# First chunk's q computed token tile by token tile and transposed by DMA, with the opening loads regrouped and GpSimd's order fixed

## The chip, the core and the metric

The kernel runs on one core of one Trainium2 chip. The metric is the device time of one execution in microseconds (us). Three runs of the kernel before took 745.28, 745.38 and 747.18 us; the median is 745.38 us.

## The reference

The input is one sequence of 2048 tokens by 1024 features, in bf16. Two residual blocks follow each other.

```python
def _A_ref(x, wqkv, wo):            # 32 heads of 32, window 8, dilation 2
    qkv = (x @ wqkv).reshape(B, S, 3, H, Dh)  # -> q, k, v
    ...
    logits = einsum('bhsd,bhswd->bhsw', q, kg) * scale   # kg: k of the tokens s, s-2, .. s-14
    o = einsum('bhsw,bhswd->bhsd', softmax(masked logits), vg)
    return o.reshape(B, S, D) @ wo
def _B_ref(x, w_in, w_sp, b_sp, w_out):
    z = gelu(x @ w_in)                        # 3584 columns: z1 | z2
    g = w_sp @ layernorm(z2) + b_sp           # mixing over the 2048 tokens
    return (z1 * g) @ w_out
h  = x + _A_ref(layernorm(x), wqkv, wo)
h2 = h + _B_ref(layernorm(h), w_in, w_sp, b_sp, w_out)
```

The change lies in the very first step: layernorm(x) and the q part of `x @ wqkv` for the first 512 tokens.

## The kernel before, in words

**Tiling.** The 2048 tokens are four chunks of 512 (`NCH`, `CH`); a chunk is four token tiles of 128 (`TPC`). The 1024 features are eight slices of 128 (`KT`). A product with 512 moving columns is one matmul instruction; 64 of them make q, k or v of one chunk.

**Opening (L202 to L267).** TensorE first runs 14 matmuls on a zero tile (`warm`, L206). SP's queue loads x tiles 0 and 1, ScalarE's queue loads tiles 3 and 2 (L210). Then SP loads wq in eight slices (L213), wk (L214), x tiles 4 to 7, wv (L217), and the other x tiles. An x buffer holds a pair of tiles, and there are four (`x4k`), so the tiles from 8 on wait until the `norm` of earlier tiles has read theirs. On GpSimd's queue the constants `csb` (among them the identity for transposes) are loaded first (L155). Each of the first four tiles goes through statistics (`stats` on VectorE; tile 3 in `stats_act` on ScalarE), a square root on ScalarE and a reciprocal (`rstd_of`), `norm`, eight transposes on TensorE and one copy out of PSUM (`xpose`). The result is `xnT[0]`, features on partitions and tokens along the free axis.

**q, k, v (`qkv`, L327).** For every chunk, weight slices are stationary and `xnT[c]` with its 512 tokens moves, so that the outcome has features on partitions. For q of chunk 0, four accumulators are filled together (L340), since a slice of wq is used as it arrives; all other groups run at L349. ScalarE copies chunk 0's q, k, v straight into `att_in[0]` (L356). For chunks 1 to 3 it copies to `stg` (L361), which SP stores to DRAM, and GpSimd's queue loads them again (L382) when the attention of the chunk before has let go of the buffers.

**Chunks 1 to 3 of x (`ln1`, L289).** VectorE takes statistics, GpSimd does one power (L298, 1/sqrt), VectorE does four `norm`s, GpSimd's queue writes them to DRAM (L304, `xn_d`), and SP brings them back transposed (`dma_start_transpose`, L309). The `xn` tiles and the `stg` tiles share four buffers.

**Attention (`attention`, L372).** VectorE multiplies q with shifted k (L405) and halves the sums (L409, L412); TensorE finishes the logits (L428); softmax runs on VectorE and ScalarE; two small matmuls spread the weights (L481); VectorE multiplies and adds over the window (L502, L508) into oT. `head` (L528) multiplies by wo (L550), adds x and normalizes. `b_z2` and `b_z1` (L623, L673) follow, and after L753 the token mixing (L771) and the output product (L788).

**What sets the order.** A planner written in the kernel (`Order`, L60) is given every operation with an engine, an assumed duration, dependences and a priority. It simulates the engines, from assumed starting clocks (L278: TensorE 12.9, ScalarE 12.0, VectorE 12.6) and assumed arrivals of x (`X_AT`, L286), and emits the operations by planned start. `manual_schedule` (L748) keeps that order on TensorE, ScalarE and VectorE. For the opening, and on SP's and GpSimd's queues throughout, a scheduler outside the kernel's text places the instructions. Every engine and every queue works strictly in its order: an instruction that waits holds up all behind it.

Of the kernel before, what the change touches and what calls it, by code (L numbers as in the profile page):

```python
# [20 lines left out]
P = 128  # L21
NT = S // P
CH = 512
# [9 lines left out]
NWARM = 14  # L33
# [7 lines left out]
def _consts():  # L41
    c = np.zeros((P, 128 + 32 + 128 + 128), np.float32)
    c[:, 0:128] = np.eye(P)
    for p in range(P):
        c[p, 128 + p // 4] = 1.0
    for k in range(P):
        h = k % 32
        c[k, 160 + 4 * h:160 + 4 * h + 4] = 1.0
    for w in range(W_WIN):
        for s in range(16):  # L50
            if s - DIL * w < 0:
                c[0:32, 288 + w * 16 + s] = NEG
    return c.astype(ml_dtypes.bfloat16)
# [70 lines left out]
def kernel(  # L124
# [18 lines left out]

    consts_d = nc.inline_tensor(_consts(), name="qt_consts")
# [16 lines left out]
    V.memset(eps_t[:], EPS)  # L161
    nhalf = cpool.tile([P, TPC], FP32, name="nhalf")
    V.memset(nhalf[:], -0.5)
# [29 lines left out]
    def x_slot(i):  # L193
        if i // 2 not in pairs:
            pairs[i // 2] = l1.tile([P, 2, D], BF16, name="xp", tag="x4k", bufs=4)
        xts[i] = pairs[i // 2][:, i % 2, :]

    def load_x(i):
        x_slot(i)
        dma(xts[i], x2d[i * P:(i + 1) * P, :])  # L200
# [4 lines left out]
    for _ in range(NWARM):  # L205
        T.matmul(wps[:], warm[:, 0:P], warm[:], start=True, stop=True)  # L206

    for i in (0, 3, 1, 2):
        x_slot(i)
        (dma if i < 2 else A.dma_start)(xts[i], x2d[i * P:(i + 1) * P, :])  # L210
    wsb = [wtile([P, KT, D], "wq", "wA"), wtile([P, KT, D], "wk", "wA"), wtile([P, KT, D], "wv", "wB")]
    for kt in range(KT):
        dma(wsb[0][:, kt, :], wq_view[:, kt, 0:D])  # L213
    dma(wsb[1][:], wq_view[:, :, D:2 * D])  # L214
    for i in range(TPC, 2 * TPC):
        load_x(i)
    dma(wsb[2][:], wq_view[:, :, 2 * D:3 * D])  # L217
    for i in range(2 * TPC, NT):
        load_x(i)
# [6 lines left out]

    def stats_act(i):
        sm = l1.tile([P, 4], FP32, name="sm", tag="sm")
        jk = l1.tile([P, D], BF16, name="jk", tag="xn", bufs=4)
        A.activation(jk[:], xts[i], ACTF.Identity, accum_out=sm[:, 0:1])  # L230
        A.activation(jk[:], xts[i], ACTF.Square, accum_out=sm[:, 1:2])
        V.tensor_scalar(mv1[:, i, 0:1], sm[:, 0:1], 1.0 / D, None, op0=ALU.mult)
        V.tensor_tensor(sm[:, 2:3], mv1[:, i, 0:1], mv1[:, i, 0:1], op=ALU.mult)
        V.scalar_tensor_tensor(mv1[:, i, 1:2], sm[:, 1:2], 1.0 / D, sm[:, 2:3], op0=ALU.mult, op1=ALU.subtract)
# [12 lines left out]

    def xpose(i, xn):
        tp = ps_acc.tile([P, KT, P], BF16, name="tpa", tag="acc")
        for a in range(KT):  # L250
            T.transpose(tp[:, a, :], xn[:, a * P:(a + 1) * P], ident)
        (V.tensor_copy if i == 2 else A.copy)(xnT[0][:, :, i * P:(i + 1) * P], tp[:])
# [3 lines left out]
    stats_act(3)  # L256
    stats(V, 0)
    rstd_of(0, 1)
    stats(V, 1)
    xpose(0, norm(0))  # L260
    rstd_of(1, 2)
    rstd_of(3, 4)
    xpose(1, norm(1))
    xpose(3, norm(3))
    stats(V, 2)
    rstd_of(2, 3)
    xpose(2, norm(2))  # L267
# [10 lines left out]
    o_ = Order({"PE": 12.9, "ACT": 12.0, "DVE": 12.6, "POOL": 12.0}, {"acc": 3, "L": 1, "prod": 2, "part": 2, "xn": 4})  # L278
# [7 lines left out]
    X_AT = {1: 18.5, 2: 27.5, 3: 30.5}  # L286
# [26 lines left out]
    att_in = {}  # L313

    def alloc_att_in(c):
        qT = att.tile([P, DLO, CH], BF16, name="qT", tag="qT")
        kT = att.tile([P, DLO, HALO + CH], BF16, name="kT", tag="kT")
        vT = att.tile([P, DLO, HALO + CH], BF16, name="vT", tag="vT")
        att_in[c] = (qT, kT, vT)

# [6 lines left out]
    def qkv(c):  # L327
        for xi in range(3):
            wv = wsb[xi][:].rearrange("p kt (m dl) -> p kt dl m", dl=DLO)
            for dp in range(DLO // 2):  # L330
                key = ("acc", "qkv", c, xi, dp)
                deps = [G.get(("xnT", c))]
                if c == 0 and xi == 0 and dp < 2:
                    def mm(wv=wv, dp=dp):
                        if dp == 0:
                            accs = [new_acc(), new_acc()]
                            G["acc", "qkv", 0, 0, 0], G["acc", "qkv", 0, 0, 1] = accs
                            for kt in range(KT):
                                for dl in range(4):
                                    T.matmul(accs[dl // 2][:, dl % 2, :], wv[:, kt, dl, :], xnT[0][:, kt, :],  # L340
                                             start=(kt == 0), stop=(kt == KT - 1))
                    last = add("PE", 6.91 if dp == 0 else 0.0, mm, deps, prio=order(), take="acc")
                else:
                    for j in range(2):
                        def mm(j=j, dl=2 * dp + j, wv=wv, key=key):
                            if j == 0:
                                G[key] = new_acc()
                            for kt in range(KT):
                                T.matmul(G[key][:, j, :], wv[:, kt, dl, :], xnT[c][:, kt, :],  # L349
                                         start=(kt == 0), stop=(kt == KT - 1))  # L350
                        last = add("PE", 1.727, mm, deps, prio=order(), take="acc" if j == 0 else None)
                        deps = [last]
                def ev(xi=xi, dp=dp, key=key):
                    if c == 0:
                        off = 0 if xi == 0 else HALO
                        A.copy(att_in[0][xi][:, 2 * dp:2 * dp + 2, off:off + CH], G[key][:])  # L356
                        if xi > 0 and dp == 3:
                            dma(qkv_d[xi][:, :, CH - HALO:CH], att_in[0][xi][:, :, CH:CH + HALO])
                    else:
                        stg = l1.tile([P, 2, CH], BF16, name="stg", tag="xn", bufs=4)  # L360
                        A.copy(stg[:], G[key][:])  # L361
                        dma(qkv_d[xi][:, 2 * dp:2 * dp + 2, c * CH:(c + 1) * CH], stg[:])
                G["ev", c, xi, dp] = add("ACT", 0.92, ev, [last], prio=2.0, free="acc", lat=0.15, take="xn" if c else None)
                if c:
                    dma_op(3.5, lambda: None, [G["ev", c, xi, dp]], free="xn")
            G["wdone", c, xi] = last
        G["qkvlast", c] = last
# [4 lines left out]
    def attention(c):  # L372
        if c == 0:
            d_q = G["ev", 0, 0, 3]
# [319 lines left out]
    alloc_att_in(0)  # L694
    V.memset(att_in[0][1][:, :, 0:HALO], 0.0)
    V.memset(att_in[0][2][:, :, 0:HALO], 0.0)
# [51 lines left out]
    with tc.manual_schedule(engines={mybir.EngineType.PE, mybir.EngineType.Activation, mybir.EngineType.DVE}):  # L748
        o_.run()
# [80 lines left out]
```

## Time and profile before

| | before |
|---|---|
| median of three runs | 745.38 us |
| span of the profiled execution (first to last instruction) | 742.7 us |
| TensorE busy | 724.7 us (98%) |
| VectorE busy | 418.2 us (56%) |
| ScalarE busy | 219.5 us (30%) |
| GpSimd busy | 50.7 us (7%) |
| DMA moved | 104.22 MB |

The page gives the profiled execution's span and no other time for it; the median of the runs is 2.7 us above the span. PE is TensorE's matmuls, PEld its weight loads, DVE VectorE, ACT ScalarE, POOL GpSimd, SP SyncE; an added q (SPq) means the queue or sequencer of that engine. In a timeline a row has its start, its length, the engine, the line, the operation, what it writes and reads, and in brackets the idle time before it and what ended that. Line numbers L are those of the kernel before.

### The profile page before, as it was taken

To read this page: it belongs to the slowest core of one execution; us is meant where nothing else is said; L and a number is where in the kernel's file an instruction comes from. 1 tells how busy PE (TensorE), PEld (TensorE's weight loads), DVE (VectorE), ACT (ScalarE), POOL (GpSimd) and SP (SyncE) were. 2 spreads that over 40 slices of the span, in tenths; PEclk is the share of its full clock that TensorE was granted. 3 is DMA by queue.
4 is the path that set the end of the run, shared out by engine and by line. 5 is a ranking of instruction groups with operands and counts; after the bars stand their busy time and mean duration, and the time that the engine had idled before them with its cause. 6 is when DMAs were issued, how large, how long until landed. Compare 5 with 4: busy or idle time off the path is not lost.

```text
span 742.7 us, 8553 instructions
## 1 busy us (share of the span) xinstructions
PE 724.7 (98%) x3535; PEld 370.0 (50%) x3598; DVE 418.2 (56%) x423; ACT 219.5 (30%) x267; POOL 50.7 (7%) x56
## 2 busy tenths in 40 slices
PE   7999999999999999999999999999999999999997
PEld 4665565566645444444445544444444444444443
DVE  4699899988999899879932012231222223212222
ACT  4332522444237954596562631000000000000000
POOL 0130200100011100200112000000000000000000
PEclk9999999999999999999999999999999999999999
DMA  8954564476493732370069578126114411020001
GB/s 345 391 149 115 171 186 129 142 214 212 156 327 94 218 117 72 114 221 21 28 222 355 151 244 274 59 76 165 51 36 101 140 57 31 26 94 20 1 27 58
DMA packets 108855, 104.22 MB, mean 140 GB/s; under 512 B 63536, under 2 KB 87376, under 8 KB 108688
## 3 DMA queue, kind: packets, MB, share of 16 engines
q1 hardware_dynamic: 101248, 71.64, 32.0%
q0 software_dynamic: 7280, 31.50, 12.1%
q8 instruction: 28, 0.46, 0.3%
q10 hardware_dynamic: 288, 0.52, 0.2%
q14 instruction: 11, 0.09, 0.0%
HBM read 55.09 MB, written 33.88 MB: 120 GB/s over the span
## 4 chain that ended last, share of the span: by engine, by line
PE 80%; DVE 11%; DMA 5%; issue 1%; ACT 1%; POOL 1%; SPq 0%; POOLq 0%; DVEq 0%; ACTq 0%
PE acc L771 26%; PE acc L349 14%; PE acc L788 12%; PE acc L623 9%; PE acc L673 8%; PE acc L550 7%; DMA xp<-in_A_x_dram 3%; DVE prod L502 2%; DVE oT L508 2%; DVE prod L405 1%; DMA wq<-in_A_wqkv_dram 1%; DVE part L409 1%; PE acc L796 1%; POOL l3rstd L522 1%; DMA xn_d_65<-xn 1%
## 5 line engine op out<-in xcount | busy, mean ns | idle before, releaser
L623 PEld LDWEIGHTS <-hnT 128*128 128x128 bf16 x512 | 49.8, 98 | 47.7 <-issue 0.9
L405 DVE TENSOR_TENSOR prod<-qT,kT 128x4096 bf16<-128x4096 bf16 x32 | 72.1, 2286 | 0.0
L788 PEld LDWEIGHTS <-zg 128*128 128x128 bf16 x420 | 41.1, 98 | 49.6
L502 DVE TENSOR_TENSOR prod<-vT,AB 128x4096 bf16<-128x4096 bf16 x28 | 63.8, 2290 | 1.0
L508 DVE TENSOR_TENSOR oT<-oT,prod 128x4096 bf16<-128x4096 bf16 x28 | 64.0, 2286 | 0.1
L623 PE MATMUL acc<-win_1420,hnT 128*128 128x512 bf16 x245 | 59.6, 379 | 0.5
L361 ACT CAST stg<-acc 128x1024 bf16<-128x1024 f32 x36 | 36.4, 1012 | 79.3 <-PE acc L349 74.3
L673 PE MATMUL acc<-hnT,win_1637 128*128 128x512 bf16 x256 | 57.6, 379 | 0.5 <-ACT z1s L679 0.5
L790 DVE TENSOR_TENSOR ot<-acc,hr 128x1024 bf16<-128x1024 f32 x15 | 18.4, 1225 | 69.4 <-PE acc L788 60.5
L349 PE MATMUL acc<-xnT,wk 128*128 128x512 bf16 x250 | 56.7, 380 | 0.3
L349 PE MATMUL acc<-xnT,wv 128*128 128x512 bf16 x252 | 56.8, 380 | 0.2
L550 PE MATMUL acc<-wo_sb,oT 128*128 128x512 bf16 x251 | 56.0, 379 | 1.0 <-DVE oT L508 0.7
L788 PE MATMUL acc<-wout_a,zg 128*128 128x512 bf16 x236 | 54.0, 379 | 0.3
L349 PE MATMUL acc<-xnT,wq 128*128 128x512 bf16 x218 | 49.2, 379 | 0.5 <-issue 0.2
L623 PE MATMUL acc<-win_1544,hnT 128*128 128x256 bf16 (+1 forms) x253 | 46.5, 325 | 0.4 <-issue 0.2
L349 PEld LDWEIGHTS <-wk 128*128 128x128 bf16 x256 | 36.4, 143 | 19.1 <-issue 0.9
L349 PEld LDWEIGHTS <-wv 128*128 128x128 bf16 x256 | 36.4, 143 | 19.1 <-issue 0.9
L673 PE MATMUL acc<-hnT,win_1643 128*128 128x512 bf16 x192 | 42.9, 379 | 0.0
L788 PE MATMUL acc<-wout_b,zg 128*128 128x512 bf16 x175 | 40.7, 379 | 0.2
L349 PEld LDWEIGHTS <-wq 128*128 128x128 bf16 x224 | 31.9, 143 | 16.8 <-issue 0.8
L550 PEld LDWEIGHTS <-oT 128*128 128x128 bf16 x256 | 24.8, 98 | 31.0 <-DVE oT L508 1.2
L630 ACT ACTIVATE u<-acc 128x1024 bf16<-128x1024 f32 (+1 forms) x32 | 29.1, 911 | 36.1 <-PE acc L623 36.1
(284 smaller groups left out, 952.3 us busy)
## 6 DMA issues: line engine op xcount, KB each, us to landing
z_d<-z1s SPq DMA_DIRECT2D x28, 256.0 KB, 2.7
z1c<-z_d SPq DMA_DIRECT2D x28, 256.0 KB, 2.8
z_d<-u SPq DMA_DIRECT2D x12, 448.0 KB, 2.8
xr<-in_A_x_dram SPq DMA_DIRECT2D x16, 256.0 KB, 3.0
h_d<-hb SPq DMA_DIRECT2D x16, 256.0 KB, 2.5
hr<-h_d SPq DMA_DIRECT2D x16, 256.0 KB, 2.8
out_dram<-ot SPq DMA_DIRECT2D x15, 256.0 KB, 2.0
xp<-in_A_x_dram SPq DMA_DIRECT2D x14, 256.0 KB, 10.1
```

What stands on the lines that cost most here:

```text
L349: T.matmul(G[key][:, j, :], wv[:, kt, dl, :], xnT[c][:, kt, :], start=(kt == 0), stop=(kt == KT - 1))
L361: A.copy(stg[:], G[key][:])
L405: V.tensor_tensor(st["prod"][:], qT[:], kT[:, :, o:o + CH], op=ALU.mult)
L502: V.tensor_tensor(pvs[w][:], vT[:, :, o:o + CH], abb, op=ALU.mult)
L508: prev = add("DVE", 2.3, lambda w=w: V.tensor_tensor(oTs[c][:], oTs[c][:], pvs[w][:], op=ALU.add), [prev, m_], prio=3.0, lat=0.15, free="p ...
L550: T.matmul(st["acc", il][:, nh, :], oTs[c][:, dl, il * P:(il + 1) * P], wo_sb[:, dl, nh * CH:(nh + 1) * CH], start=(dl == 0), stop=(dl == ...
L623: T.matmul(accf[:, n0:n1], hnTs[c][:, il, kt, :], wins[hf][:, kt, n0:n1], start=(kt == 0), stop=(kt == KT - 1))
L630: A.activation(st["u", il][:, hf * 1024:hf * 1024 + wd], G["accz", c, il, hf][:].rearrange("p a b -> p (a b)")[:, 0:wd], ACTF.Gelu_apprx_t ...
L673: T.matmul(G["accy", c, fp][:, j, :].rearrange("p (a b) -> p a b", a=TPC), wt[:, kt, f0 * P:(f0 + 1) * P], hnTs[c][:, :, kt, :], start=(kt ...
L771: T.matmul(acc[:, j, :], z2sb[a][:, f * P:(f + 1) * P], wspT[:, a, :], start=(a == 0), stop=(a == NT - 1))
L788: T.matmul(acc[:, nh, :], zg[:, f, il * P:(il + 1) * P], wt[:, f0, nh * CH:(nh + 1) * CH], start=(f == 0), stop=(f == NF - 1))
L790: V.tensor_tensor(ot[:], acc[:].rearrange("p a b -> p (a b)"), hr[:], op=ALU.add)
```

## The change

- **q of chunk 0** no longer goes through `qkv`. For each of the four token tiles, `xpose` brings the normalized tile into `xnT[0]`, and `q_part` then multiplies with the x tile stationary and wq moving (8 feature slices by 2 halves of 512 columns, 16 matmuls a tile). So the outcome has tokens on partitions. ScalarE copies it, with columns reordered, to `qs`, and four DMA transposes on SP's queue (`q_out`) put it into `att_in[0]`. The matmuls of a tile are cut in two (`cut` 4, 6, 5, 8 of 8 slices), and the next tile's transposes stand between the parts.
- **All four first tiles** are treated alike, in the order 0, 1, 2, 3, with statistics on VectorE. The copy out of PSUM is halved between ScalarE and VectorE.
- **Opening loads** are all on SP, in a fixed order: x0, two slices of wq, x1, the other wq in three pairs of slices, x tiles 2 and 3 as one load, 4 and 5, wk, 6 to 11 in pairs, wv, 12 to 15 in pairs.
- **The fixed order** holds from the start of the kernel on, and on GpSimd too. In the built program the load of `wo_sb` (2 MB), which stood second on GpSimd's queue, comes after the `xn_d` writes of chunk 2. The power of chunk 3 (L298) comes after the load of q of chunk 1 and not before it, and the `xn_d` writes of chunk 3 stand two by two around the load of k of chunk 1. On SP the four q transposes stand after the last x load and before the transpose of chunk 1 (L309).
- **The planner** starts from other clocks and arrivals, and chunk 0 takes q as ready at 39.0. The order it emits is new all the way. On VectorE the statistics of two of chunk 3's tiles come after the products of q and k of chunk 0 instead of before them. There is one warm-up matmul more.

```diff
-NWARM = 14
+NWARM = 15
...
+    ctx_order = tc.manual_schedule(engines={mybir.EngineType.PE, mybir.EngineType.Activation,
+                                            mybir.EngineType.DVE, mybir.EngineType.Pool})
+    ctx_order.__enter__()
...
-    for i in (0, 3, 1, 2):
-        x_slot(i)
-        (dma if i < 2 else A.dma_start)(xts[i], x2d[i * P:(i + 1) * P, :])
...
-    for kt in range(KT):
-        dma(wsb[0][:, kt, :], wq_view[:, kt, 0:D])
-    dma(wsb[1][:], wq_view[:, :, D:2 * D])
-    for i in range(TPC, 2 * TPC):
-        load_x(i)
-    dma(wsb[2][:], wq_view[:, :, 2 * D:3 * D])
-    for i in range(2 * TPC, NT):
-        load_x(i)
+    def load_wq(k):
+        dma(wsb[0][:, 2 * k:2 * k + 2, :], wq_view[:, 2 * k:2 * k + 2, 0:D])
+
+    with tc.manual_schedule(engines={mybir.EngineType.SP}):
+        for i in range(2):
+            x_slot(i)
+        dma(xts[0], x2d[0:P, :])
+        load_wq(0)
+        dma(xts[1], x2d[P:2 * P, :])
+        for k in range(1, KT // 2):
+            load_wq(k)
+        load_pair(1)
+        load_pair(2)
+        dma(wsb[1][:], wq_view[:, :, D:2 * D])
+        for k in (3, 4, 5):
+            load_pair(k)
+        dma(wsb[2][:], wq_view[:, :, 2 * D:3 * D])
+        for k in (6, 7):
+            load_pair(k)
...
+    def prep(i):
+        stats(V, i)
+        rstd_of(i, i + 1)
+        return norm(i)
+
     def xpose(i, xn):
-        tp = ps_acc.tile([P, KT, P], BF16, name="tpa", tag="acc")
+        tp = ps_acc.tile([P, 2, 2 * CH], BF16, name="tpa", tag="acc")
         for a in range(KT):
-            T.transpose(tp[:, a, :], xn[:, a * P:(a + 1) * P], ident)
-        (V.tensor_copy if i == 2 else A.copy)(xnT[0][:, :, i * P:(i + 1) * P], tp[:])
+            T.transpose(tp[:, a // 4, (a % 4) * P:(a % 4 + 1) * P], xn[:, a * P:(a + 1) * P], ident)
+        for hf, cp in ((0, A.copy), (1, V.tensor_copy)):
+            cp(xnT[0][:, 4 * hf:4 * hf + 4, i * P:(i + 1) * P], tp[:, hf, 0:CH].rearrange("p (a s) -> p a s", a=4))
+
+    def q_part(i, lo, hi):
+        if lo == 0:
+            qacc[i] = new_acc()
+        for kt in range(lo, hi):
+            for nh in range(2):
+                T.matmul(qacc[i][:, nh, :], xnT[0][:, kt, i * P:(i + 1) * P], wsb[0][:, kt, nh * CH:(nh + 1) * CH],
+                         start=(kt == 0), stop=(kt == KT - 1))
+
+    def q_out(i):
+        A.copy(qs[:, i], qacc[i][:].rearrange("p a (m dl) -> p dl a m", dl=DLO))
+        nc.sync.dma_start_transpose(att_in[0][0][:, :, i * P:(i + 1) * P], qs[:, i])
...
-    stats_act(3)
-    stats(V, 0)
...
-    xpose(2, norm(2))
+    xpose(0, prep(0))
+    for i, cut in enumerate((4, 6, 5, KT)):
+        q_part(i, 0, cut)
+        if i < TPC - 1:
+            xpose(i + 1, prep(i + 1))
+            q_part(i, cut, KT)
+        q_out(i)
...
-    o_ = Order({"PE": 12.9, "ACT": 12.0, "DVE": 12.6, "POOL": 12.0}, {"acc": 3, "L": 1, "prod": 2, "part": 2, "xn": 4})
+    o_ = Order({"PE": 21.8, "ACT": 22.6, "DVE": 17.5, "POOL": 12.0}, {"acc": 3, "L": 1, "prod": 2, "part": 2, "xn": 4})
...
-    X_AT = {1: 18.5, 2: 27.5, 3: 30.5}
+    X_AT = {1: 18.0, 2: 22.5, 3: 36.0}
...
-        for xi in range(3):
+        for xi in range(0 if c else 1, 3):
...
-            d_q = G["ev", 0, 0, 3]
+            d_q = add("DMA", 39.0, lambda: None)
...
-    with tc.manual_schedule(engines={mybir.EngineType.PE, mybir.EngineType.Activation, mybir.EngineType.DVE}):
-        o_.run()
+    o_.run()
+    ctx_order.__exit__(None, None, None)
```

## The prediction

> **What bounds the kernel now.** I read the engines' busy time first, then TensorE's waits, then the timelines of the opening and of VectorE, and last the rows of the DMA transposes. The page:
>
> ```profile
> PE 724.7 (98%) x3535; PEld 370.0 (50%) x3598; DVE 418.2 (56%) x423; ACT 219.5 (30%) x267; POOL 50.7 (7%) x56
> ```
>
> TensorE is idle for 18.0 of 742.7 us. Its work stays the same (64 matmuls for q of chunk 0 before and after, 32 transposes, one more warm-up), so the change can only move the end by those idle microseconds and by the clock of the opening. TensorE's timeline of the first 32 us:
>
> ```profile
> 1.26 5.42 PE L206 MATMUL wps<-warm 128*128 128x512 bf16 x14 [1.26 <-DVE warm L203]
> 9.10 3.53 PE L251 MATMUL tpa<-csb,xn 128*128 128x128 bf16 x32 [2.42 <-DVE xn L243]
> 13.51 7.10 PE L340 MATMUL acc<-xnT,wq 128*128 128x512 bf16 x31 [0.88 <-DVE xnT L252]
> ...
> 27.35 4.91 PE L349 MATMUL acc<-xnT,wk 128*128 128x512 bf16 x22
> ```
>
> The reader is to see that q occupies TensorE from 13.51 to 27.35 without a gap, and that before it stand a wait of 2.42 us for the first normalized tile and transposes at 107 ns apiece (3.53 us over 32). TensorE's waits in the first 100 us, without the one for the warm-up tile:
>
> ```profile
> PE L L428 <- DVE part L412: 2.5, 2, 1.4
> PE tpa L251 <- DVE xn L243: 2.4, 1, 2.4
> ...
> PE acc L340 <- DVE xnT L252: 0.9, 1, 0.9
> PE pb L481 <- DVE attn L469: 0.3, 1, 0.3
> ```
>
> The logits of chunk 0 wait twice for VectorE (1.35 and 1.18 us). VectorE's timeline from 77 us shows a wait of its own just ahead of the third:
>
> ```profile
> 83.34 0.55 DVE L243 TENSOR_SCALAR xn<-xp,mv_75,rstd_76 128x1024 bf16<-128x1024 bf16 x1 [1.81 <-DMA xn_d_65<-xn]
> ```
>
> After 100 us TensorE hardly waits, until the 3.4 us that follow its last matmul.
>
> **Step 1, the opening.** Terms from rows: a full-clock matmul takes 0.216 (64 from 27.35 to 41.17); eight transposes 0.45 when the clock is full (L590, 392.11 to 392.56), first one's start to last one's end 0.61; a half copy about 0.5 on ScalarE (L252: 0.95 for a whole one) and 0.35 on VectorE. From arrival to a normalized tile: statistics 1.54 (22.69 to 24.23), square root 0.09 + 0.30, reciprocal and norm 0.08 + 0.08 + 0.54, in all 2.65.
>
> The first x tile's statistics start at 4.54 now, while four x tiles share the DMA engines. Alone in front it comes earlier, at most by the three other tiles' 0.79 MB at 0.39 MB per us (the 385 to 391 GB/s of 14 to 20 us), 2.0 us; I take 4.0. It is normalized at 6.65. The 15 warm-ups start 0.15 earlier, as their tile is now VectorE's first memset, and end near 6.75. So the 2.42 us of waiting vanish. Transposes 6.75 to 7.2, copies to 7.9, first part of q (8 matmuls, 1.73) 7.95 to 9.7. VectorE takes up tile 1 after its copy at 7.75 and is done at 10.4: TensorE waits 0.7. From there q parts cover VectorE (4.3 us of matmuls against 3.4 for tile 2) up to tile 3, where 0.3 is lost. Sum: 6.75 + 13.82 (q) + 1.8 (transposes) + 1.8 (gaps) = 24.2, against 27.35: **3.15 earlier**. If no gap remained, 22.4; if each of the four tiles takes VectorE 0.8 more, the gain is gone (27.4).
>
> The weights must come in time: after x0 at 4.0, with 0.52 MB a load, wq's pairs of slices land at 5.4, 7.4, 8.7 and 10.0 and are wanted at 7.95, 8.4, 10.9 and 11.8; x tiles 2 and 3 land at 11.4, wanted at 11.5. This holds because `wo_sb` leaves: it is issued at 1.96 and lands at 12.5 now, and the slices of wq take 9.5 to 10.6 from issue to landing beside it. If it still shared the engines, 2.1 MB would add 5.4 and the gain would be gone. x as stationary operand costs nothing: its weight load (98 ns at L623, 143 for wq's strided slices) hides under 216. The copy to `qs` is bounded by 0.95 (L252) and 1.23 (L486); I take L356's 1.01. ScalarE does it between square roots, and the one that it delays by 0.65 (tile 2) is covered by the same matmuls.
>
> **The clock.** The windows of one microsecond from 9 to 13 have granted clocks of 0.60, 0.50, 0.50 and 0.69, after TensorE had idled from 6.68 to 9.10; the other windows from 13 us on have 1.00. The new opening leaves no idle stretch over 0.75 us, shorter than the 1.35 us of 60 us, which lowered no clock, so I cost it at full clock. Bounds: 0 to 3.4 us at half clock, 1.7 lost. The Trainium skill, "TensorE: Matmul & The Clock Gate", Part 1, says that the clock halves after an idle window of about 3.4 us, of a window that runs free. The trace differs, since it halved after 2.42 us idle; by that rule the phase alone could still halve it, and the sum would be 1.7 worse.
>
> **Step 2, x of the other chunks and the four DMA transposes.** VectorE is free of the first tiles at 20.05. Chunk 1: statistics 5.75 (22.69 to 28.44), GpSimd's power 1.04, during which one tile of chunk 2 (1.5) goes through, norms 1.92: 29.4. Each x load from the sixth pair on waits on SP for norms of two tiles, so the last two are issued at about 28.5 and 29.5, and the q transposes, ready since 25.2, stand behind them. Nearest row for their price, 1 MB from SBUF, in four pieces here and one there:
>
> ```profile
> L597 SPq DMA_TRANSPOSE hnT<-hb x3: 4721/4803/4831, 151.6 to 317.4; - x3
> ...
> DMA to landing us min/median/max: 6.7/6.7/6.8
> ```
>
> Four quarters at 1.2 issue and a common tail: 29.95 + 6.7 = 36.7, and 2 more for the 1 MB of x ahead and the `xn_d` writes: 38.7. The upper end is four full ones in a row, 29.95 + 26.8 = 56.7. I take the lower, as L597 issues its 1 MB in one piece in 4.8 of its 6.7. The Trainium skill, "VectorE: DVE Perf Modes", The three transpose paths, speaks against it: 1309 ns for a 128 by 128 block by DMA against 390 on TensorE; for 32 blocks in a row that would be an estimate of 41.9 us, q at 72. The row's 32 blocks in 6.7 us disagree.
>
> Chunk 2 on VectorE: three tiles 4.3, power 1.3, norms 1.9: 37.2; two tiles of chunk 3, 2.95: 40.2. k is out of PSUM at 24.2 + 13.82 + 1.2 = 39.2. So VectorE starts the products at **40.2 instead of 45.78**, 5.6 earlier, and 2.95 of statistics come later.
>
> **Step 3, what TensorE waits for next.** Half of the parts takes 15.85 (45.78 to 61.63): ready at 56.1. TensorE comes to the first logits after v (51.85) and 40 matmuls: 60.5, no wait. Second half ready at 71.8; TensorE there at 60.5 + 0.55 + 56 x 0.216 = 73.1, no wait. The spread matmul follows 48 matmuls later, at 84.0; VectorE gets there from 71.8 with 2 statistics (2.9) and two norms (1.1), and the softmax's rows (78.66 to 81.5, then 83.8 to 87.0), at 82.3: no wait. The waits of 1.35 + 1.18 + 0.27 = 2.8 go; I count **2.5**. VectorE's 1.81 at 83.34 came from GpSimd's queue: its `xn_d` writes stood behind the load of q of chunk 1, issued at 74.86. The first writes of chunk 3 now follow that load too, but the buffer they free is wanted only at 92, after the first sums of oT.
>
> What is late next: the transpose of chunk 1 must land before 51.85, when v is done. Its source lands near 36.3 (last write issued 30.5, 5.1 to 6.5 to landing), then 5.9 alone. It meets 1 MB of `xn_d` for chunk 2 and now the 2 MB of `wo_sb`, issued at 38.3: 4.2 MB from 38.5 at 0.39 is 49.3, and 0.5 MB of x for the residual makes 50.6. Slack 1.2, where before it was 6 (landing at 48.9, wanted at 54.98). I cost it at 0 and keep 3 for the range. After the last `head`, the new order leaves no matmuls between the transposes at L590 and L623, where there were 16; VectorE's copies took until 395.4, 0.85 after the last transpose, so 0.5 is lost. Waits from 100 to 450 us sum to some 3.4; the order is new there, and I leave them as they are, with 2 to both sides.
>
> **Sum.** 742.7 - 3.15 - 2.5 + 0.5 = 737.5 for the span, 5.15 less. The median lies 2.7 above the span, and 745.38 - 5.15 gives **740.2**.
>
> **Rivals.**
> 1. *More is gained*: no gaps in the opening (22.4 instead of 24.2) and the later waits shrink by 2: 736.4. For it: the starting clocks in the new planner leave room for it. Against: VectorE's chain of 3.7 us a tile is as long as TensorE's work for it.
> 2. *Only the opening pays, or less*: VectorE, busy 10 of 10 us from 50 to 70, stays as late against TensorE as before, the waits of 2.5 remain, and a half clock costs up to 1.7: 742.7 to 744.4, the latter no change. Against: 5.6 us of lead on VectorE against 3.15.
> 3. *Slower*: the q transposes in SP's queue cost a full 6.7 each. Then q lands at 56.7 and the transpose of chunk 1, right behind, at 62.6, while TensorE is through with v at 51.85 and idles 10.8, with a half clock afterwards (1.7). q of chunk 1 starts at 62.6 instead of 54.98; 7.6 + 1.7 + 0.5 - 2.5: 752.7. It turns slower by the bound from a landing at about 59 on, as 51.85 + 5.15 + 2.2 = 59.2.
> 4. *The change doesn't do what it says*: the order in which the engines' instructions stand shows that it does, but if `csb` (issued 1.23, landing 5.1 later, at 6.3) came 3 us later, the first transposes would wait for the identity and step 1's gain would be gone: 743.4.
>
> **How the numbers follow.** A change within 0.3% (2.2 us, 743.1 to 747.6) can't be told from none. Forecast 0.58, rival 1 0.14, rival 2 0.16 (half faster, half same), rival 3 0.07, rival 4 0.05 (same, or slower where clock and gap add up, a fifth). Faster: 0.58 + 0.14 + 0.08 = 0.80; same 0.12; slower 0.08. The range goes from rival 1's 736.4 to 743.6, which takes in a half clock with half of the waits (740.2 + 1.7 + 1.3 = 743.2) and leaves out rival 3 and the upper end of rival 2.
>
> **What would show it.** k's first matmul near 24.2 and clock 1.00 from 7 us on (step 1); four q transposes from about 30 that land before 40, and products at 40.2 (step 2); no wait over 0.5 at the three rows before 90 us, and chunk 1's q directly after v (step 3). Wrong would make it a late slice of wq, a long idle stretch at 52, or new waits between 100 and 450 us.

## The result and the profile after

Five runs of the changed kernel took 749.46 to 766.37 us, median 750.04; five of the kernel before, beside them, 744.61 to 747.18, median 745.28. The ratio is **1.0075, interval 1.0055 to 1.0096**: slower by 0.75%, where 740.2 was forecast. The ratios in this document leave out runs that count as slow, here the one of 766.37. The profiled execution of the changed kernel took 755.16 us (span 753.4), so what is read from its trace below is a loss some 5 us larger than that of the median run.

The page of the kernel after gives the engines' busy time. TensorE's records of the trace before lack 63 matmuls (3535, where one fewer than the 3599 of after is due), so the busy sums can't be subtracted; starts of rows can.

```profile
PE 731.5 (97%) x3599; PEld 365.9 (49%) x3599; DVE 421.1 (56%) x426; ACT 217.9 (29%) x264; POOL 47.8 (6%) x56
```

TensorE's timeline of the kernel after, the rows that answer to those of before (start, length, engine, line, operation; in brackets the idle time before and what ended it):

```profile
1.19 5.38 PE L208 MATMUL wps<-warm 128*128 128x512 bf16 x15 [1.19 <-DVE eps_t L209]
6.41 0.61 PE L272 MATMUL tpa<-csb,xn 128*128 128x128 bf16 x8
7.69 2.17 PE L284 MATMUL acc<-wq,xnT 128*128 128x512 bf16 x8 [0.68 <-ACT xnT L274]
...
25.20 13.98 PE L362 MATMUL acc<-xnT,wk 128*128 128x512 bf16 x64
39.02 13.98 PE L362 MATMUL acc<-xnT,wv 128*128 128x512 bf16 x64
61.57 11.32 PE L362 MATMUL acc<-xnT,wq 128*128 128x512 bf16 x40 [8.58 <-DMA xnT<-xn_d]
74.10 0.62 PE L440 MATMUL L<-part,csb 128*32 128x512 bf16 x8 [1.21 <-DVE part L424]
...
89.86 0.62 PE L440 MATMUL L<-part,csb 128*32 128x512 bf16 x8 [2.90 <-DVE part L424]
90.41 7.09 PE L362 MATMUL acc<-xnT,wk 128*128 128x512 bf16 x24
```

The opening did become shorter: k starts at 25.20, 2.15 earlier. Then v is done at 53, and chunk 1's q has no input until 61.57. And 40 matmuls of that q take 11.32 where 40 at full clock take 8.86 (105.14 us, the same trace), 24 of k 7.09 instead of 5.34. The table of windows shows why (for each stretch its length, PE busy and matmuls, granted clock, DMA share as the sum of packet times, which can pass 1, and GB/s):

```profile
40.00:56.00 16.00, 12.99 (x61) 1.00 1.09 231
56.00:62.00 6.00, 0.43 (x1) 0.53 1.11 238
62.00:67.00 5.00, 5.00 (x14) 0.54 1.13 243
67.00:90.00 23.00, 18.89 (x96) 1.00 0.28 83
90.00:94.00 4.00, 4.00 (x17) 0.57 0.43 160
```

The clock is halved behind the wait of 8.58 and again behind that of 2.90. What was waited for is on SyncE's queue. These are its rows for q's transposes (L289) and for those of the chunks (L341): first how long SyncE took to issue one (least, median, most, in nanoseconds) and when the first and the last were issued, below that the time from issue to landing in microseconds. Before them stands the row of chunk 1's transpose in the kernel before.

```profile
L309 SPq DMA_TRANSPOSE xnT<-xn_d_63 x1: 5082/5082/5082, 39.3 to 39.3; - x1
```
```profile
L289 SPq DMA_TRANSPOSE qT<-qs x4: 1947/3596/6682, 31.2 to 40.6; - x4
...
DMA to landing us min/median/max: 7.6/13.3/18.7
```
```profile
L341 SPq DMA_TRANSPOSE xnT<-xn_d x3: 3952/4465/11961, 47.4 to 118.1; - x3
...
DMA to landing us min/median/max: 6.4/6.5/14.1
```

The fourth of q's transposes landed at 57.98 and not at 38.7. Behind it in the queue, chunk 1's was issued at 47.4, took 11.96 to issue instead of 5.08, and landed at 61.52. VectorE, with nothing else to do, started its products 12.4 later than before:

```profile
58.20 4.50 DVE L417 TENSOR_TENSOR prod<-qT,kT 128x4096 bf16<-128x4096 bf16 x2 [16.20 <-DMA qT<-qs]
```

**The balance.** By the first spread matmul (`pb`, 87.11 before, 102.61 after) the kernel after has done 16 matmuls more, 3.46, so at equal work it is 12.05 behind: -2.15 opening, +8.58 for chunk 1's transpose, +1.31 for logits (4.11 against 2.8), +2.46 and +1.75 at half clock, which is 11.95, all but 0.1. From there to the end it is 1.35 faster: the waits of 1.32 at 324 us (logits) and 0.75 at 371 us (oT) are gone, one of 0.30 is new. That would make 1.77; what takes 0.4 of it back was not followed. 12.05 - 1.35 = 10.7, the difference of the spans.

### The profile page after: what moved, and what is told of

It is laid out like the page before. It is cut to its first block, busy times and chain, and to the rows that moved or that the text cites. A ratio compares the mean times of both kernels' runs of the same rounds, so it can differ in the third digit from the quotient of the medians.

```text
span 753.4 us, 8614 instructions
## 1 busy us (share of the span) xinstructions
PE 731.5 (97%) x3599; PEld 365.9 (49%) x3599; DVE 421.1 (56%) x426; ACT 217.9 (29%) x264; POOL 47.8 (6%) x56
## 4 chain that ended last, share of the span: by engine, by line
PE 81%; DVE 10%; issue 3%; DMA 2%; ACT 1%; POOL 1%; DVEq 0%; ACTq 0%; POOLq 0%
PE acc L780 26%; PE acc L362 13%; PE acc L797 12%; PE acc L685 11%; PE acc L635 10%; PE acc L562 6%; DVE prod L417 3%; DMA qT<-qs 2%; DVE prod L514 2%; DVE oT L520 1%; DVE prod L421 1%; PE acc L284 1%; PE acc L805 1%; PE wps L208 1%; DVE part L424 1%
## 5 line engine op out<-in xcount | busy, mean ns | idle before, releaser
L780 PE MATMUL acc<-wspT,z2sb 128*128 128x512 bf16 x896 | 194.0, 379 | 0.0
L780 PEld LDWEIGHTS <-z2sb 128*128 128x128 bf16 x896 | 87.7, 98 | 105.7
L783 DVE TENSOR_TENSOR g<-acc,bB 128x1024 bf16<-128x1024 f32 x28 | 34.3, 1224 | 159.8 <-PE acc L780 134.1
L685 PE MATMUL acc<-hnT,win 128*128 128x512 bf16 x448 | 99.4, 379 | 0.4 <-ACT z1s L691 0.4
L635 PE MATMUL acc<-win,hnT 128*128 128x512 bf16 (+1 forms) x512 | 98.5, 352 | 0.0
L685 PEld LDWEIGHTS <-win 128*128 128x128 bf16 x448 | 43.3, 98 | 52.6 <-issue 1.9
L362 PE MATMUL acc<-xnT,wk 128*128 128x512 bf16 x256 | 58.9, 388 | 0.0
L362 PE MATMUL acc<-xnT,wq 128*128 128x512 bf16 x192 | 45.4, 395 | 8.6 <-DMA xnT<-xn_d 8.6
L362 PEld LDWEIGHTS <-wk 128*128 128x128 bf16 x256 | 36.7, 145 | 20.5 <-issue 2.9
L642 ACT ACTIVATE u<-acc 128x1024 bf16<-128x1024 f32 (+1 forms) x32 | 29.2, 914 | 38.3 <-PE acc L635 38.3
```

The costliest lines, as they stand in the source:

```text
L635: T.matmul(accf[:, n0:n1], hnTs[c][:, il, kt, :], wins[hf][:, kt, n0:n1], start=(kt == 0), stop=(kt == KT - 1))
L642: A.activation(st["u", il][:, hf * 1024:hf * 1024 + wd], G["accz", c, il, hf][:].rearrange("p a b -> p (a b)")[:, 0:wd], ACTF.Gelu_apprx_t ...
L685: T.matmul(G["accy", c, fp][:, j, :].rearrange("p (a b) -> p a b", a=TPC), wt[:, kt, f0 * P:(f0 + 1) * P], hnTs[c][:, :, kt, :], start=(kt ...
L780: T.matmul(acc[:, j, :], z2sb[a][:, f * P:(f + 1) * P], wspT[:, a, :], start=(a == 0), stop=(a == NT - 1))
L783: V.tensor_tensor(g1[:], acc[:], bB[:, c * CH:(c + 1) * CH].unsqueeze(1).to_broadcast([P, 2, CH]), op=ALU.add)
```

## The experiments

**Theory**: the load of `wo_sb` (2 MB, issued at 40.0 on GpSimd's queue, 17.0 us to landing where it took 10.5 in the kernel before) and the transposes hold each other up. **Rivals**: the place of q's transposes behind the last two x loads is enough by itself; or it is the size of `wo_sb`'s packets, or its queue. Times below stand beside runs of the kernel before on the same chip (medians 744.85 to 745.55).

### 1. `wo_sb` moved later or earlier

In the kernel after, the load goes behind chunk 1's q load on GpSimd's queue (`e1_wo_late`, shown here; it was issued at 86.8 us), or second on the queue as in the kernel before (`e2_wo_early`, at 1.9):

```diff
+            if c == 1:
+                dma_op(8.0, lambda: dma_w(wo_sb[:], ...), [d_q])
...
-    dma_op(8.0, lambda: dma_w(wo_sb[:], ...), [G["wdone", 0, 2]])
```

> The changed kernel with one edit: wo_sb (2 MB) is loaded behind the load of chunk 1's q on GpSimd's queue, some 78 us, instead of at 40.0. Theory T: the DMA transposes stall because wo_sb's 16 KB packets share the DMA engines with them. Then the four q transposes land by 46 (57 to 58 in the changed kernel), the products start by 46 instead of 58.2, chunk 1's q follows v at 53 without a wait (8.6 now), and the time is 741 to 744. Rival R1: four small transposes are slow by themselves, or behind the x loads and the xn_d writes; then the products start at 52 or later, TensorE still waits 3 us or more at 53, and the time is 747 to 750. Rival R2: the new order of the instructions costs the time; then the wait goes and the time is still 746 or more.

> The changed kernel with wo_sb loaded second on GpSimd's queue at 2 us, as in the kernel before. Theory T: the transposes run free, products by 48 and no wait of TensorE before chunk 1's q; but the slices of wq and the x tiles share the DMA engines with it from 5 to 12 us, so that k starts up to 5 us later than 25.2, at 27 to 30; 744 to 748. Rival R1: products at 52 or later on top of the late opening, 751 or more. Rival R2: 748 or more without waits.

Late: **748.84**, 1.005 [1.0026, 1.0073]. q landed at 46.23, chunk 1's transpose at 51.67, and chunk 1's q waited for nothing. So the 8.6 came from `wo_sb`'s traffic. The time missed theory T's 741 to 744 and fits rival R2 (the new order costs the time); experiment 3 decides against R2. TensorE's waits show what came next:

```profile
PE L L442 <- DVE part L426: 3.4, 2, 2.9
PE acc L362 <- ACT stg L373: 3.4, 1, 3.4
```

The 2.9 is for VectorE, whose products began at 46.45 when q came. The 3.4 is put down to the moved load: it runs from 86.8 to 95.6, and ScalarE waits 5.3 for stores that must free a buffer of `stg`. Early: **748.42**, 1.0051 [1.0033, 1.0069]. TensorE waits 4.4 for wq and k starts at 30.66, but chunk 1's q waits for nothing. The products began at 52.82, where 48 was expected, and the logits waits are 4.5 in all. Both places avoid the collision and pay elsewhere.

### 2. Packet size, and the kernel before with the late load

> The changed kernel with wo_sb loaded at the same place in eight DMAs of 256 KB, whose packets are 2 KB instead of 16 KB; the bytes are the same. Theory T in its narrow form, that the size of the packets stalls the transposes: products by 50, the wait at 53 under 3 us, 743 to 747. If the bytes alone do it: as the changed kernel, products at 56 to 58, wait 7 to 9, 749 to 750. R1: no difference either, 749 to 750.

`e3_wo_2k` (the kernel after, `wo_sb` in eight loads of 256 KB, packets of 4 KB instead of 16 KB; 2 KB was expected): **756.41**, 1.0149 [1.0131, 1.0168]. Chunk 1's q waits 11.6, q's slowest transpose took 20.5 to landing. It doesn't take packets of 16 KB.

> The kernel before with GpSimd's queue in the planner's order and wo_sb behind the load of chunk 1's q (some 85 us); q as before, no q transposes, loads as before. If the opening's contention with wo_sb is what makes VectorE late in the kernel before, x of chunk 1 comes up to 5 us earlier than 22.7, the products start 2 to 5 us earlier than 45.8, TensorE's waits for the logits (2.8 us) go, and the time is 741 to 744: most of what the change was predicted to gain without its q. If not, 745.

`e4_before_wo_late` (the kernel before, GpSimd in the planner's order, `wo_sb` at 80.9): **744.8**, 0.9992 [0.9981, 1.0003]. x of chunk 1 comes 5 us earlier, both logits waits of chunk 0 go, and a wait of 2.2 for `stg` comes. So these logits waits go without any change to q, but the time (741 to 744 expected) hardly moved: in its trace k starts 1.3 later (28.67) and the new wait takes 2.2.

### 3. `wo_sb` held until 61 us, and q's transposes first

A one-column ScalarE copy into `wo_sb` behind chunk 1's second copy of q makes the load wait (`f1_wo_held`). `f2_wo_held_q_first` also puts q's transposes ahead of the last two x loads; `f3_q_first` does that alone.

```diff
                         A.copy(stg[:], G[key][:])
+                        if (c, xi, dp) == (1, 0, 1):
+                            A.copy(wo_sb[:, 0, 0:1], stg[:, 0, 0:1])
...
-    dma_op(8.0, lambda: dma_w(wo_sb[:], ...), [G["wdone", 0, 2]])
...
+    dma_op(8.0, lambda: dma_w(wo_sb[:], ...), [G["ev", 1, 0, 1]])
```
```diff
         dma(wsb[2][:], wq_view[:, :, 2 * D:3 * D])
-        for k in (6, 7):
-            load_pair(k)
...
         q_out(i)
+    for k in (6, 7):
+        load_pair(k)
```

> The kernel after, with wo_sb's load held on GpSimd's queue until chunk 1's second copy of q out of PSUM (about 61 us), so that it lies neither beside chunk 1's transpose (as at 40) nor beside the stores of chunk 1 to 2 (as at 78). Theory A (wo_sb beside the transposes is the whole loss): q's transposes land near 41, VectorE's products start near 42, no wait before chunk 1's q, no wait for logits, about 741. Theory B (two causes; the transposes of q stand behind the last two x pairs on SyncE's queue and beside the stores of xn too): q lands at 45 to 47 as with the load at 78, no wait before chunk 1's q, the 3.4 us wait for stg is gone, but a logits wait of some 2.9 us and its half clock stay; 745 to 747.

> The kernel after, with wo_sb's load held until about 61 us and the four transposes of q ahead of the last two x loads on SyncE's queue. Theory B: q lands at 28 to 38, the products start at 40 to 42, where kT or VectorE's norms are last, no wait before chunk 1's q, no wait for logits of over 0.5 us: 745.5 - 2.15 (opening) - 2.5 (logits) + 0.5 = 741.3, 740 to 743. Theory C (the transposes of q are slow wherever they stand, since the stores of xn run beside them): q lands at 45 or later, the logits wait stays, 745 to 747. Against both: the last two x pairs now land later, and chunk 1's transpose behind them; if that takes over 52 us, a wait before chunk 1's q comes back, 746 or more.

> The kernel after, with the four transposes of q ahead of the last two x loads on SyncE's queue, and wo_sb's load where it was (about 40). Theory B: q lands before 38 and the products start near 42, but chunk 1's transpose still meets wo_sb and lands at 54 to 62: a wait of 1 to 8 us before chunk 1's q, 744 to 749. Theory A (wo_sb's traffic is all): q is no longer beside it, the rest as in Theory B. Theory D (the place on SyncE's queue is all): 741 to 742, with no wait before chunk 1's q.

`f1_wo_held`: **741.95** (740.91 to 744.66), 0.9954 [0.994, 0.9968]. This one operation moved takes 8.1 off the kernel after and lands 1.8 above the forecast. The time is that of theory A, the path that of B: q still lands at 45.57 and the logits wait is still there. The rows of q's transposes and of the chunks', then TensorE's longest wait:

```profile
L289 SPq DMA_TRANSPOSE qT<-qs x4: 1570/3367/3460, 30.7 to 39.2; - x4
...
DMA to landing us min/median/max: 6.3/6.9/8.4
```
```profile
L341 SPq DMA_TRANSPOSE xnT<-xn_d x3: 4077/4269/4482, 42.9 to 103.9; - x3
...
DMA to landing us min/median/max: 6.1/6.3/8.1
```
```profile
PE L L442 <- DVE part L426: 3.4, 2, 2.9
```

What B had wrong is the price: its sum left out the 1.35 of later waits that are gone, and the same 2.90 idle is followed by full clock here. The windows around it (as above):

```profile
74.00:77.00 3.00, 0.55 (x3) 1.00 0.32 78
77.00:81.00 4.00, 3.34 (x21) 1.00 0.60 208
81.00:85.00 4.00, 4.00 (x21) 1.00 0.19 66
```

`f2_wo_held_q_first`: **742.38**, spread over 738.29 to 747.08, 0.995 [0.9921, 0.9979]. In the profiled run (738.29, the shortest) the products start at 43.22 (40 to 42 was expected) with no wait for q, and no logits wait is over 0.3. What is late next is chunk 1's transpose; its slowest, 11.9 to issue, lands at 52.99, 0.4 after TensorE wants it:

```profile
L341 SPq DMA_TRANSPOSE xnT<-xn_d x3: 4002/4365/11934, 37.5 to 101.6; - x3
...
DMA to landing us min/median/max: 6.0/6.4/15.5
```

`f3_q_first`: **769.31** (761.04 to 776.52), 1.0282 [1.0212, 1.0351], far outside what any theory had given. Chunk 1's transpose is now issued at 36.3, just ahead of chunk 2's stores (36.7 to 38.5) and of `wo_sb` at 39.05. In the profiled run, the longest, all of them crawl (the stores land at 64.5 to 83.9, `wo_sb` at 89.0); the three others, 761.04 to 771.87, have no trace:

```profile
L341 SPq DMA_TRANSPOSE xnT<-xn_d x3: 4563/4787/46530, 36.3 to 139.8; - x3
...
  PE acc L362: 37.5, 1
...
DMA to landing us min/median/max: 6.6/6.8/53.7
```

From 45 to 82 us of that trace, the DMA table (for each queue: packets, MB, share of the 16 engines' time):

```profile
DMA packets 2212, 3.06 MB, mean 83 GB/s; under 512 B 1903, under 2 KB 1903, under 8 KB 2104
...
q1 hardware_dynamic: 1838, 0.47, 74.1%
q0 software_dynamic: 373, 2.58, 43.5%
```

The engines are counted as busy throughout, yet SyncE's queue (q1, the transpose) moves 0.47 MB in 37 us. By the packet records, a 256-byte packet of the transpose takes 18 ns when it is alone (1,130 a microsecond over all engines at 57 to 60 us of the kernel after). Here two in three still take under 30 ns, but one in eight takes some 0.62 us and one in sixteen some 1.25, one or two times the 0.61 of a 16 KB packet of `wo_sb`; 50 a microsecond get through.

The Trainium skill, "DMA: Bandwidth & Descriptors", "Queues, rings and completion order", says that each DMA engine takes turns between its queues, a packet at a time. The times of the slow fifth of the small packets agree. The turns do not explain the rest: 2.9 packets of 16 KB a microsecond passed as well, where 16 engines at 0.61 would pass 26 (an estimate, 16 / 0.61). Why both crawl is open.

### 4. The kernel before with the same load held

> The kernel before, with GpSimd's queue in the planner's order and wo_sb's load held until about 61 us; q is still made with xnT moving and not transposed. Theory B: the waits for logits are gone as with the load at 83, and the 2.15 us wait for stg at 86 to 88 is gone too: 742 to 744. Rival: the load at 61 delays x's stores of chunk 2 instead and a wait of 2 us comes up elsewhere: 744 to 746.

**744.26**, 0.9988 [0.997, 1.0005]. The logits wait at 323 us, which the kernel before has too, and 1.7 for `stg` are left; theory B wanted the latter gone, and the time fits the rival. Without the rest of the change, moving the load gives 1.3, and the interval takes in no change. The remaining 2.3 of what `f1_wo_held` gains belong to the rest of the change together: the new q, the regrouped loads and the new order, which no run takes apart.

### 5. Which queue, which traffic, how many transposes

`g1_before_wo_at_38` and `h1_before_wo_at_28` are the kernel before with GpSimd in the planner's order and the load right behind chunk 2's or chunk 1's x stores. `g2_wo_on_act_queue` and `h2_wo_on_sync_queue` are the kernel after with the load on ScalarE's queue (first diff) or SyncE's (second), behind k's last copy out of PSUM:

```diff
                         A.copy(att_in[0][xi][:, 2 * dp:2 * dp + 2, HALO:HALO + CH], G[key][:])
+                        if (xi, dp) == (1, 3):
+                            nc.scalar.dma_start(wo_sb[:], ...)
...
-    dma_op(8.0, lambda: dma_w(wo_sb[:], ...), [G["wdone", 0, 2]])
```
```diff
+                        if (xi, dp) == (1, 3):
+                            A.copy(wo_sb[:, 0, 0:1], att_in[0][1][:, 0, HALO:HALO + 1])
+                            dma(wo_sb[:], ...)
...
-    dma_op(8.0, lambda: dma_w(wo_sb[:], ...), [G["wdone", 0, 2]])
```

> The kernel before, GpSimd's queue in the planner's order and wo_sb's load right behind chunk 2's stores of xn (about 38), beside the transpose of chunk 1 on SyncE's queue (34 to 43 without it). q is still made with xnT moving and not transposed, so this is the regrouped queue alone. Theory E (GpSimd's traffic stalls any DMA transpose beside it, also without q's four): chunk 1's transpose lands well behind 43, and where it passes 54.8 TensorE waits for xnT; 745 to 765. Rival (it takes the transposes of q in the queue as well): chunk 1's transpose lands by 50, no wait, the logits waits are gone: 743 to 745.

**745.05**, 0.9997 [0.9981, 1.0014], with the transpose landed at 45.0: the rival's figures. But the run told less than it was meant to: the transpose's small packets ran from 35.4 to 39.6, the first of GpSimd's stores came at 39 and those of `wo_sb` from 42 on. They hardly met.

> The kernel after, with wo_sb's 2 MB issued by ScalarE on its own hardware queue at about 39 in place of GpSimd's queue at 40: the same bytes at the same time. Theory E (it is GpSimd's queue that stalls the transposes): q lands at 45 to 50, chunk 1's transpose by 53 to 56, wait before chunk 1's q under 3 us: 742 to 747. Rival (any 2 MB beside the transposes does it): q lands near 58 and chunk 1's q waits about 8 us as in the kernel after: 749 to 753.

**750.98** (748.54 to 770.99), 1.0052 [1.0028, 1.0076]. Even the shortest run is above theory E's 742 to 747, so E fell: it doesn't take GpSimd's queue. Only the longest run has a trace; there q's transposes took up to 35.4 to land.

> The kernel before, GpSimd's queue in the planner's order and wo_sb's load right behind chunk 1's stores of xn (about 28), so that its packets are on the DMA engines before chunk 1's transpose (issued at about 34) and not behind it, as they were with the load at 38. No transpose of q. Theory G (any DMA transpose whose packets meet a large load of another queue is stalled, however many transposes there are): the transpose takes 10 us or more to issue, lands at 50 to 65 (43 to 45 before), wo_sb takes 15 us or more, and TensorE waits for xnT where it passes 54.8; 745 to 757. Rival H (it takes several transposes in flight, as q's four make them): lands by 47, no wait for xnT, 743 to 746.

**745.23**, 1.0005 [0.9988, 1.0023]. Now they met, and a single transpose was enough:

```profile
L311 SPq DMA_TRANSPOSE xnT<-xn_d x3: 3752/3976/15928, 33.5 to 106.1; - x3
...
DMA to landing us min/median/max: 5.8/6.0/21.2
```

It landed at 54.73 and was wanted at 56.43, so nothing was lost in time. `wo_sb` had landed at 40.67, so from there on only chunk 2's x stores (issued 34.5 to 36.8, landed 49.4 to 51.7) were beside it: 1 MB of stores in 4 KB packets can do it too. They don't always: in `e4_before_wo_late` and `f4_before_wo_held` the same stores were issued 1 us behind the same transpose, most of its packets passed before theirs, and it landed in 9.4 and 9.1.

> The kernel after, with wo_sb's load on SyncE's own queue behind chunk 1's transpose, so that its packets stand behind the transposes' in one queue. Theory G (packets of two queues interleave on the same DMA engines; one queue goes in order): no transpose meets wo_sb; q lands at 45 to 47, chunk 1's transpose at about 51, no wait before chunk 1's q; a logits wait of 2.9 us stays, and chunk 2's transpose and vT are later by wo_sb's time without cost: 740 to 745. Rival I (2 MB at that time stalls the transposes from any queue): q lands near 58 and the wait before chunk 1's q is over 5 us: 749 to 757.

**743.14**, 0.9976 [0.9962, 0.9989]: the same 2 MB, only 9 us later and behind the transposes in their own queue. q landed at 46.05, chunk 1's transpose at 51.42; TensorE waited for neither, VectorE 5.2 for q, as in `f1_wo_held`. So theory G held, though the later hour and the queue were changed together; no run has the load at 49 on GpSimd's queue. Chunk 2's transpose, right behind the load in the same queue, landed in 9.6. What hurts is other queues' traffic beside a transpose. The logits wait of 2.9 stayed, here with a half clock behind it (0.57 from 79 to 83 us, 1.00 before).

### 6. Chunk 2's stores held, and the two copies out of PSUM

`g3_stores_held` takes `f2_wo_held_q_first` and holds chunk 2's stores behind a GpSimd copy that waits for ScalarE's second copy of v; `g4_two_psum_tiles` also gives each half of an x tile's transposes its own PSUM tile.

```diff
+                        if (xi, dp) == (2, 1):
+                            A.copy(hold[:], eps_t[:])
...
+                if c == 2 and il == 0:
+                    nc.gpsimd.tensor_copy(hold2[:], hold[:])
                 dma_w(xn_d[c][il * P:(il + 1) * P, :], ...)
...
```
```diff
-        tp = ps_acc.tile([P, 2, 2 * CH], BF16, name="tpa", tag="acc")
+        tp = [ps_acc.tile([P, 2, 2 * CH], BF16, name="tpa", tag="acc") for _ in range(2)]
...
```

> The kernel with wo_sb's load held until about 61 us and q's transposes first on SyncE's queue, and now also chunk 2's four stores of xn held on GpSimd's queue until about 46 us (a GpSimd copy that waits for ScalarE's second copy of v). Theory E: chunk 1's transpose, which took 11.9 us to issue beside those stores and landed at 53.0, issues in 4 to 5 us and lands near 45; the wait before chunk 1's q (0.4) goes and the runs lie closer together (738 to 741, where they were spread over 738 to 747): median 738.5 to 740. Rival (the transpose is slow there for the last two x pairs, not for the stores): it still lands at 50 or later, 741 to 743. Against both: stg's buffers are free later, a wait for stg near 56 to 60 of under 2 us.

**739.23** (738.42 to 740.39), 0.9907 [0.9888, 0.9926]. Chunk 1's transpose took 7.4 to issue, not the 4 to 5 expected (the last two x pairs still stand right ahead of it in its own queue; that they are the cause is not shown), and landed at 46.29. The spread of 8.8 us over nine runs became 2.0 over five. One logits wait of 1.7 came back.

> The kernel with chunk 2's stores held, and the halves of each x tile's transposes in two PSUM tiles, so that VectorE's copy waits for TensorE and not for ScalarE's copy. Theory F (the opening fell short because the two copies out of PSUM ran one behind the other): the copies start together, each of the four tiles saves 0.3 to 0.5 us, k starts at 23.5 to 24.2 where it was 24.7 to 24.9; 0.5 to 1.2 us less than without the second tile. Rival (x's arrival or the norm sets the opening): k starts at 24.7 to 24.9 as before, time unchanged within 0.4.

**736.76** (736.51 to 737.24), 0.9874 [0.9854, 0.9895]: the fastest of all, 8.5 under the kernel before and 13.3 under the kernel after. ScalarE's and VectorE's copies of the first tile, in this kernel:

```profile
6.69 0.59 ACT L274 COPY xnT<-tpa 128x512 bf16<-128x512 bf16 x1 [1.27 <-PE tpa L272]
6.91 0.42 DVE L274 COPY xnT<-tpa 128x512 bf16<-128x512 bf16 x1 [0.72 <-PE tpa L272]
```

In the kernel after VectorE's copy waited for ScalarE's although they touch different halves:

```profile
7.67 0.42 DVE L274 COPY xnT<-tpa 128x512 bf16<-128x512 bf16 x1 [1.54 <-ACT xnT L274]
```

With two PSUM tiles it starts beside it, and k starts at 23.83. ScalarE's copy gains as well: it starts 0.44 after the first transpose instead of 0.64, as its tile now has four transposes and not eight. Theory F held, with 2.5 saved where 0.5 to 1.2 was expected: 1.2 in the opening (25.04 with one tile), and 1.2 in the logits wait (1.7 to 0.5), as VectorE is earlier too.

## Why the prediction was wrong, step by step

- **Step 1, k at 24.2, 3.15 earlier.** The mechanism was right, the size short by a third: 25.20, 2.15 earlier (24.7 to 25.4 in the later experiments with one PSUM tile and the load out of the opening, 1.95 to 2.6 earlier). The mis-sized term is the two half copies taken as parallel: they ran one behind the other, 0.58 + 0.42, until the PSUM tile was split, which gives 23.83. x0's statistics started at 3.5 (taken: 4.0) and the first norm was done at 6.1 (6.65), so that was not the lack. "This holds because `wo_sb` leaves" was right as well: with the load back in the opening, TensorE waits 4.4 for wq and k starts at 30.66, 5.5 later, by the working's own 5.4.
- **The clock.** The opening ran at 1.00 from its first full window on, as costed. The bound of 1.7 was used for the opening alone; the price fell 50 us later, 2.46 and 1.75 behind the new idle stretches. The same idle of 2.90 was followed by 24 matmuls in 7.09 (half clock) in the kernel after, `e1_wo_late`, `e3_wo_2k` and `h2_wo_on_sync_queue`, and by full clock in `e2_wo_early` and `f1_wo_held`. So no idle time of that length can be called safe. The free-running window that the step quotes from the skill agrees with such a difference between runs; its length of about 3.4 us does not agree with halving after 2.90.
- **Step 2, q at 38.7 and VectorE's products at 40.2.** This is the step that failed: 57.98 and 58.20. The working took one transpose's 6.7 us (L597) as the price of four and added 2 us for the 1 MB of x and the writes around them, 8.7 in all. In place of that the runs showed two prices. Behind the last x loads and beside the stores of xn alone, the four take 14.9 to 15.2 from first issue to last landing; q lands at 45.6 to 46.2 and VectorE waits 4 to 5 us. With `wo_sb` on the same engines they take 26.8, 12 more. Without its wait for q VectorE would have been ready at 40.8 to 42.5 (58.20 - 16.20 in the kernel after, 45.79 - 5.03 in `f1_wo_held`, 46.45 - 4.00 in `e1_wo_late`), 0.6 to 2.3 after the 40.2; where q's transposes stand ahead of the last x loads it starts at 41.8 to 44.3, after a wait of 2.2 to 3.3 for x of chunk 3. The estimate of 41.9 us for 32 blocks, drawn from the skill, was rightly set aside: with hardly any other traffic, a megabyte lands in 5.8 to 6.8. The printed parts of the working add up to 29.2 and 36.9 where it has 29.4 and 37.2; that changes nothing here.
- **Step 3, slack of 1.2 at chunk 1's transpose.** The `wo_sb` load was seen to lie beside it, but the price was worked out from bytes, 4.2 MB at 0.39 MB per us: 50.6. It was 61.52, a wait of 8.58 where 0 was costed and 3 kept for the range. Beside other traffic the transposes' 256-byte packets showed no fixed rate: the same 1 MB took 6 us with hardly any, 9 to 11 where most of its packets passed before the stores', 14 to 21 among stores or the load, and 54 in the worst run. Among the kernels with the new q, the 2.5 for logits came only with q early *and* the load out of the way (`f2_wo_held_q_first`, `g4_two_psum_tiles`). The 0.5 after the last `head` was not lost (0.34 of waiting there, 0.33 before), and the later waits shrank by 1.35, within the 2 kept open for them.
- **The sum.** Of the forecast's 5.15, 3.6 was there to be had: `f1_wo_held`, with nothing but the load moved, gives 741.95 beside 745.55, inside the range. The working named the load, its hour and its neighbour, and priced the meeting at nothing.
- **The rivals.** Rival 3 had the right victim and place (q at 56.7, chunk 1's transpose at 62.6; measured 57.98 and 61.52) for the wrong reason, and that its four times 6.7 is the 26.8 measured is luck: q's transposes don't add up to that where `wo_sb` is out of the way (14.9 to 15.2). At 7 in 100 it was held too unlikely; the profiled 755.16 stands beside its 752.7. Rival 2's waits for logits did remain (4.11 in the kernel after), but were not the main loss. Rivals 1 and 4 did not come: `csb` was not waited for, and only versions with further edits go below 740.

**What stays open.** The runs show that other queues' traffic stalls the transposes, from GpSimd's queue and from ScalarE's, with packets of 4 and of 16 KB, and that a load behind them in their own queue doesn't. They don't show why both sides crawl at once, nor why the size varies so much between kernels with the same neighbours and between runs of one kernel (748.54 to 770.99).

## What to carry to other kernels

A moved load is a change of its own: list what its transfer will lie beside at its new hour, and don't price a DMA transpose by bytes when any other queue is moving data beside it. Put a large load behind the transposes in their own queue (743.14 here), or hold it with a tiny write into its destination until they are through (741.95). Where two engines copy halves out of one PSUM tile, look in the timeline whether the second really starts with the first.

## What the runs showed of the hardware that was not expected

- A DMA transpose of 1 MB landed in 5.8 to 6.8 us with hardly any other traffic, in 9.1 to 9.4 with 1 MB of stores from GpSimd's queue issued 1 us behind it (`e4_before_wo_late`, `f4_before_wo_held`), in 15.5 among such stores (right behind the last x loads, `f2_wo_held_q_first`), in 21.2 beside the tail of a 2 MB load and those stores (`h1_before_wo_at_28`), and in 53.7 beside both at once (`f3_q_first`). The load itself took 17.0 in the kernel after and 49.9 in `f3_q_first`, against 8.7 behind the transposes in their own queue and 8.2 held until 61 us.
- In `f3_q_first`, from 45 to 85 us, the DMA share was 0.98 to 1.33 in every stretch of 5 us and the rate 36 to 139 GB/s, against 289 for the transpose alone (57 to 60 us of the kernel after, share 1.27). So a full DMA row in the profile doesn't tell the rate.
- The same idle time of TensorE, 2.90 us at the same instruction, was followed by a half clock in the kernel after, `e1_wo_late`, `e3_wo_2k` and `h2_wo_on_sync_queue` and by none in `e2_wo_early` and `f1_wo_held`.
